# One core, attention + gated FFN + spatial FFN: w3's word conversion in other slots of a tile, and VectorE's low part of x ahead of its low part of g

## The chip, the cores and the metric

The program runs on one core of a Trainium2 chip. A core has TensorE (matrix products into PSUM), VectorE, ScalarE, GpSimd and SyncE, each with a queue of its own that it works off in order; SyncE's queue issues the DMAs here. The metric is the device time of one execution in microseconds (us), the median of several runs. Rows of the profile call the engines PE (PEld: its weight loads), DVE, ACT, POOL and SP.

## What is computed

```python
# attention: chunks of 64 tokens, 8 heads of 64, 8 x 576 tokens
scores = scale * q_c @ k_c.T;  attn = softmax(scores);  x = attn @ v_c      # -> (B, S, 512)
# first FFN (moe): w_in 512x1024, three-tap convolution over tokens, w_out 1024x512
h = relu(x @ w_in)
conv = cw[0]*h[t-1] + cw[1]*h[t] + cw[2]*h[t+1]
x2 = (h * sigmoid(conv)) @ w_out
# second FFN (moe2): w_in 512x1024 (the kernel's w3), spatial product over tokens, w_out
h = relu(x2 @ w3);  u, v = halves of h;  v_n = layernorm(v)
out = (u * (w_spatial @ v_n + b_spatial)) @ w_out
```

Some of the weights arrive as 64-bit words and are turned into fp32 on the chip.

## The kernel before

Products that need full precision are made of three fp32r products: each operand is kept as a high part (a cast on ScalarE) and a low part (operand minus high part, a subtraction, `split_lo`, line 80). So x becomes `xh` and `xl`, the gated activation g becomes `gh` and `gl`, the weights `w1h`/`w1l`, `w2h`/`w2l`, `w3h`/`w3l`.

**Phase A** does attention and the first FFN on ten tiles of 512 tokens (the last two have 256), each in `KF` = 8 slots, one per 128 columns of the hidden layer. Slot s belongs to tile s // 8. The order of every engine's queue is the order in which the Python code emits the instructions (a manual schedule). A slot of the main loop (s from 9 on) emits:

- `moe_in(s)`: TensorE makes h (12 matmuls, line 467) in one of the two PSUM buffers with the tag `h`;
- `moe_h(s)`: ScalarE's ReLU `hh` (line 487), the middle tap `c` (491), small edge columns `m` (502), then VectorE's two outer taps (506);
- one slot later `moe_tanh` (ScalarE, 515 and 517) and `moe_g` (VectorE, 521); two slots later `moe_split`: `gh` on ScalarE (529), `gl` on VectorE (80); three slots later `out`, `moe_out`: 12 matmuls with w2 into the accumulators `acc` (554). After a tile's last column block ScalarE empties the four accumulators (561); that falls at the end of slots 26, 34, 42, 50, 58 and 66.

In every fourth slot (from slot 23 to slot 55 those with s % 4 == 3) TensorE also makes the scores `s` of one attention group and the product with v, `x` or `px`, of the group before. Call this a **front slot** where the product stands at the slot's head (`front` in the code): slots 16, 20, 23, 27, 31, ..., 55, 59 and 67. There `values(s)` returns two parts: `xs[0]`, ScalarE's two casts `xh` (line 432), and `xs[1]`, VectorE's two subtractions `xl`. The product takes **both** `h` buffers of PSUM; `moe_in(s)` of the same slot writes the buffer of the product's first half, so its first matmul needs the first of the two `xl` to be done. On TensorE the order in a front slot is product, scores, `out`, `moe_in`, and then the next slot's `moe_in`.

A group's softmax runs on VectorE in the front slot and the one behind it. From slot 23 on, the attention matrix is transposed by VectorE (329) and moved by 16 small DMAs per group, `pt<-t` (line 339), on SP's queue; the product four slots later reads `pt`.

**w3's conversion** goes through `later`, an object of class `Pieces`, eight pieces of 128x512 words: `load` (a DMA into one of two `raw` buffers), `scale` (ScalarE, line 91, `nr<-raw`), `merge` (VectorE, lines 95 and 99), `split` (a cast to `w3h` on ScalarE, line 147, and GpSimd's subtraction `w3l`, line 80). Before the change a piece is scaled at the end of a slot with s % 4 == 1, merged in the next slot, and split four slots after that, ahead of the next piece's merge. Phase B (second FFN) follows and is not touched.

Lines of the main loop that matter, from before:

```python
            elif s > 2 * KF and s % 4 == 1:
                later.scale()
            elif s > 2 * KF and s % 4 == 2:
                later.split()
                weave(later.merge())
                later.load()
```

Of the kernel before, what the change touches and what calls it, by code (L numbers as in the profile page):

```python
# [22 lines left out]
KF = FF // 128  # L23
# [49 lines left out]
def attention_moe_kernel(ctx: ExitStack, tc: tile.TileContext, qT, kT, vL, vP, eye, w1, cw, w2, w3, wsp, wsr, bsp, w4, out):  # L73
# [33 lines left out]
    def weave(*lists):  # L107

        for i in range(max(map(len, lists), default=0)):
            for steps in lists:  # L110
                if i < len(steps):
                    steps[i]()
# [56 lines left out]
    def w_in_pieces(w, wh, wl, order):  # L169
        cs = [slice(f * 128, f * 128 + 128) for f in order]  # L170
        return [(w[:, :, c], KD, 128, wh[:, :, c], wl[:, :, c]) for c in cs]
# [5 lines left out]
    def phase_a(mid):  # L177
# [105 lines left out]
        def att_sm1(*halves):  # L283
            weave(*[sm1_steps(*x) for x in halves])

        def att_exp(g, j):
            _, nu = size(g)
            d = att[g]
            e = d["e", j][:, :nu, :]
            if (g, j) in ACC:  # L290

                ps, mx = d["ps"][j], d["mx", j]
                sm = d["sm", j] = ap.tile([128, 8, 1], F32, tag="sm", name="sm", bufs=4)
                for i in range(nu):
                    nc.scalar.activation(
                        out=e[:, i, :], in_=ps[:, i, :], func=AF.Exp, scale=SCALE, bias=mx[:, i, :],
                        accum_out=sm[:, i, :],
                    )
                return
            nc.scalar.activation(out=e, in_=e, func=AF.Exp, scale=SCALE)  # L300
# [42 lines left out]
        def att_sm2(*halves):  # L343
            weave(*[sm2_steps(*x) for x in halves])
# [113 lines left out]
        def moe_in(s):  # L458
            i, f = divmod(s, KF)
            xh, xl = xt[i]  # L460
            w = width(i)
            ph = ps_h.tile([128, 512], F32, tag="h", name="h")[:, :w]
            terms = ((w1h, xh), (w1l, xh), (w1h, xl))
            n = 0
            for wt, x in terms if s > KF or s == 0 else (terms[0], terms[2], terms[1]):
                for k in range(KD):
                    nc.tensor.matmul(  # L467
                        ph, wt[:, k, f * 128:(f + 1) * 128], x[:, k, :w], start=n == 0, stop=n == 11
                    )
                    n += 1  # L470
            hs[s] = ph

        def moe_hh(s):
            i, f = divmod(s, KF)
            h = mp.tile([128, WMAX + 2], F32, tag="hh", name="hh", bufs=3)
            if i:
                nc.gpsimd.tensor_copy(out=h[:, 0:2], in_=carry[:, f, :])
            hhs[s] = h
# [33 lines left out]
        def moe_tanh(s):  # L512
            _, c = gs[s]
            for dst, src, w, m in fixes.pop(s):
                nc.scalar.activation(out=dst, in_=src, func=AF.Identity, scale=w, bias=m)  # L515

            nc.scalar.activation(out=c, in_=c, func=AF.Tanh, scale=0.5)  # L517

        def moe_g(s):
            h, c = gs.pop(s)  # L520
            nc.vector.scalar_tensor_tensor(out=c, in0=c, scalar=1.0, in1=h, op0=ALU.add, op1=ALU.mult)  # L521
            gs[s] = c

        def moe_split(s):
            g = gs.pop(s)
            n = outputs(s // KF)[1]
            gh = mp.tile([128, WMAX], F32R, tag="gh", name="gh", bufs=LAG)[:, :n]
            gl = mp.tile([128, WMAX], F32R, tag="gl", name="gl", bufs=LAG)[:, :n]
            nc.scalar.copy(out=gh, in_=g)  # L529
            split_lo(nc.vector, gl, g, gh)  # L530
            gs[s] = (gh, gl)
# [3 lines left out]
        def store():  # L535
            while stores:
                dst, src = stores.pop(0)
                nc.sync.dma_start(out=dst, in_=src)
# [116 lines left out]
        def scores(s):  # L655
            if s in at:
                g = at[s]
                att_s(g)((0, 1))
                if s > 1:
                    load_qk(g + 1)  # L660
                for j in range(2):
                    if s < START:
                        todo.setdefault((s, 1), []).append((g, j))
                        todo[s + 1, 2 + j] = [(g, j)]
                        todo[s + 1, 8] = [(g, 0)]
                        todo[s + 2, 4] = [(g, 1)]
                        if g < NP:
                            todo[s + 2, 5 + j] = [(g, j)]
                    else:
                        todo[s + j, 0] = (g, j)  # L670
                        if g < NP:
                            todo[s + 1 + j, 7] = (g, j)

        def values(s):
            if s in pv_at:
                g = pv_at[s]
                xs = att_pv(g)
                load_v(g + VBUFS)
                return xs
            return (lambda: None,) * 2  # L680
# [61 lines left out]
        def out(s):  # L742
            if s - LAG0 < KF:
                moe_out(s - LAG0)
            elif s - LAG >= KF:
                moe_out(s - LAG)

        for s in range(NS + LAG):
            if s < START:
                start_slot(s)  # L750
                continue
            if s == START:
                es_st.close()
            if s == 2 * KF + 1:
                es_wf.close()
                w3p = es_b.enter_context(tc.tile_pool(name="w3p", bufs=1, side="right", reuse_waits="tile"))
                for nm in ("w3h", "w3l"):
                    wB[nm] = w3p.tile([128, KD, FF], F32R, name=nm)
                es_lp = ExitStack()
                lp = es_lp.enter_context(tc.tile_pool(name="later", bufs=1, side="right"))  # L760
                later = Pieces(lp, w_in_pieces(w3, wB["w3h"], wB["w3l"], (4, 5, 6, 7, 0, 1, 2, 3)))
                later.load()


            if s < NS:
                moe_hh(s)
            xs = ()
            tp = todo.pop((s, 7), None)
            front = pv_at.get(s, 0) >= PAIRED
            if front:  # L770
                xs = values(s)
                xs[0]()
            scores(s)
            store()
            soft = todo.pop((s, 0), None)
            if KF + 2 <= s < NS + 2:
                moe_split(s - 2)
            if xs:
                xs[1]()
            if s < NS + 1:  # L780
                moe_tanh(s - 1)
            if soft:
                att_sm1(soft)
                att_exp(*soft)
            if s < NS + 1:
                moe_g(s - 1)
            if soft:
                att_sm2(soft)
            if front:
                out(s)  # L790
            if s < NS:
                moe_in(s)
                if tp:
                    tp = att_tp(*tp)
                moe_h(s)
                if tp:
                    tp()
            if not front:
                out(s)
                for x in values(s):  # L800
                    x()
            if s == NS + LAG - 1:
                store()
            if first.wait:
                first.part(*first.wait.pop(0))
            elif s > 2 * KF and s % 4 == 1:
                later.scale()
            elif s > 2 * KF and s % 4 == 2:
                later.split()
                weave(later.merge())  # L810
                later.load()
            if s == NS - KF:
                es_at.close()
                es_lp.close()
                mid()
                x2p = es.enter_context(tc.tile_pool(name="x2p", bufs=1))
                x2s = [f for b in range(2) for f in x2_parts(b, x2p)]
                x2l = [f() for f in x2s[:2]]
                x2s = x2s[2:]
            elif NS - KF < s <= NS:  # L820
                x2l.pop(0)()
                if x2s:
                    x2l.append(x2s.pop(0)())
# [6 lines left out]
    def mid():  # L830
        wB["x"] = es_b.enter_context(tc.tile_pool(name="xB", bufs=2, side="right", reuse_waits="tile"))
# [217 lines left out]
    with tc.manual_schedule():  # L1049
        phase_a(mid)  # L1050
        phase_b()
# [59 lines left out]
```

## Time and profile before

| what | value |
|---|---|
| median of 3 runs | 924.49 us (924.35 to 924.71) |
| the profiled execution, its own time | 925.31 us |
| its span, first to last instruction | 923.5 us |
| mean granted TensorE clock | 0.994 |
| busy: PE, DVE, ACT, POOL | 897.5, 574.5, 476.9, 75.0 us |
| phase A ends, phase B's first product starts | 499.96 us |

Busy times are unions of an engine's instructions over the span. TensorE is the busiest engine by far, so the reading is about the few stretches in which it waits, who ended those waits, and what the engine named had done until then.

### The profile page before, as it was taken

To read this page: it belongs to the slowest core of one execution; us is meant where nothing else is said; L and a number is where in the kernel's file an instruction comes from. 1 tells how busy PE (TensorE), PEld (TensorE's weight loads), DVE (VectorE), ACT (ScalarE), POOL (GpSimd) and SP (SyncE) were. 2 spreads that over 40 slices of the span, in tenths; PEclk is the share of its full clock that TensorE was granted. 3 is DMA by queue.
4 is the path that set the end of the run, shared out by engine and by line. 5 is a ranking of instruction groups with operands and counts; after the bars stand their busy time and mean duration, and the time that the engine had idled before them with its cause. 6 is when DMAs were issued, how large, how long until landed. Compare 5 with 4: busy or idle time off the path is not lost.

```text
span 923.5 us, 17174 instructions
## 1 busy us (share of the span) xinstructions
PE 897.5 (97%) x6820; PEld 762.1 (83%) x6820; DVE 574.5 (62%) x1061; ACT 476.9 (52%) x1046; POOL 75.0 (8%) x200
## 2 busy tenths in 40 slices
PE   6989899999999999999999999999999999999998
PEld 5656687877777777877899999989898999989897
DVE  5795887888888787875766772734527071633522
ACT  4563777767676766676566543333324233332322
POOL 0000241001111110000011110100001000100000
PEclk9899999999999999999999999999999999999999
DMA  9551313434353533321224502030020302020001
GB/s 306 177 206 46 114 48 114 138 115 137 110 155 113 154 90 89 99 68 46 65 77 139 168 14 85 13 110 23 35 64 1 119 14 84 14 80 1 29 19 57
DMA packets 64592, 81.62 MB, mean 88 GB/s; under 512 B 7680, under 2 KB 51840, under 8 KB 64384
## 3 DMA queue, kind: packets, MB, share of 16 engines
q1 hardware_dynamic: 64512, 80.53, 27.7%
q8 instruction: 54, 0.88, 0.4%
q14 instruction: 26, 0.21, 0.1%
HBM read 54.29 MB, written 18.87 MB: 79 GB/s over the span
## 4 chain that ended last, share of the span: by engine, by line
PE 69%; DVE 15%; ACT 10%; DMA 3%; SPq 2%; issue 2%; ACTq 0%
PE pss L985 13%; PE h L467 11%; PE psu L951 11%; PE pso L1004 11%; PE psv L899 11%; PE acc L554 10%; DVE c L506 4%; DVE e L320 1%; DVE sm L311 1%; ACT x L561 1%; DVE gl L80 1%; ACT c L517 1%; ACT c L515 1%; DVE e L277 1%; ACT e L300 1%
## 5 line engine op out<-in xcount | busy, mean ns | idle before, releaser
L506 DVE SCALAR_TENSOR_TENSOR c<-hh,nr,c 128x512 f32<-128x512 f32 (+3 forms) x160 | 111.8, 699 | 41.5 <-ACT c L491 38.4
L987 DVE TENSOR_TENSOR gf<-pss,bb 128x288 f32<-128x288 f32 x64 | 29.0, 452 | 146.4 <-PE pss L985 146.4
L467 PE MATMUL h<-xh,w1h 128*128 128x512 f32 (+1 forms) x320 | 84.8, 387 | 7.2 <-DVE xl L80 6.3
L467 PE MATMUL h<-xh,w1l 128*128 128x512 f32 (+1 forms) x320 | 81.5, 377 | 0.0
L467 PE MATMUL h<-xl,w1h 128*128 128x512 f32 (+1 forms) x320 | 81.4, 376 | 0.0
L989 ACT CAST gth<-gf 128x288 fp32r<-128x288 f32 x64 | 27.7, 433 | 96.3 <-DVE gf L988 96.3
L467 PEld LDWEIGHTS h<-xh,w1h 128*128 128x128 f32 x320 | 56.1, 190 | 23.6 <-DVE xl L80 10.0
L985 PE MATMUL pss<-wsh,vl 128*128 128x288 f32 x256 | 75.4, 295 | 0.0
L985 PE MATMUL pss<-wsh,vh 128*128 128x288 f32 x256 | 75.4, 294 | 0.0
L985 PE MATMUL pss<-wsl,vh 128*128 128x288 f32 x256 | 75.3, 294 | 0.0
L554 PE MATMUL acc<-gh,w2h 128*128 128x512 f32 (+2 forms) x288 | 74.8, 379 | 0.1
L554 PE MATMUL acc<-gh,w2l 128*128 128x512 f32 (+2 forms) x288 | 71.5, 370 | 0.0
L554 PE MATMUL acc<-gl,w2h 128*128 128x512 f32 (+2 forms) x288 | 71.4, 370 | 0.0
L521 DVE SCALAR_TENSOR_TENSOR c<-c,hh 128x512 f32<-128x512 f32 (+2 forms) x80 | 50.7, 634 | 27.9 <-ACT c L517 27.4
L467 PEld LDWEIGHTS h<-xh,w1l 128*128 128x128 f32 x320 | 57.8, 191 | 12.2
L467 PEld LDWEIGHTS h<-xl,w1h 128*128 128x128 f32 x320 | 57.7, 191 | 12.1
L80 DVE TENSOR_TENSOR gl<-c,gh 128x512 fp32r<-128x512 f32 (+2 forms) x72 | 50.9, 706 | 19.9 <-ACT gh L529 19.9
L487 ACT ACTIVATE hh<-h 128x512 f32<-128x512 f32 (+1 forms) x80 | 43.6, 545 | 30.4 <-PE h L467 30.2
L515 ACT ACTIVATE c<-hh,m,nr 128x1 f32<-128x1 f32 x112 | 37.6, 385 | 42.0 <-DVE c L506 42.0
L554 PEld LDWEIGHTS acc<-gl,w2h 128*128 128x128 f32 x288 | 50.8, 188 | 10.2
L554 PEld LDWEIGHTS acc<-gh,w2l 128*128 128x128 f32 x288 | 50.8, 188 | 9.9
L955 ACT ACTIVATE u<-psu 128x288 f32<-128x288 f32 x64 | 26.4, 413 | 62.5 <-PE psu L951 62.5
(126 smaller groups left out, 1876.3 us busy)
## 6 DMA issues: line engine op xcount, KB each, us to landing
raw<-in_w_dram SPq DMA_DIRECT2D x26, 512.0 KB, 5.6
x2f<-x2d SPq DMA_DIRECT2D x32, 288.0 KB, 3.2
q<-in_qT_dram SPq DMA_DIRECT2D x16, 512.0 KB, 4.5
k<-in_kT_dram SPq DMA_DIRECT2D x16, 512.0 KB, 5.5
out_dram<-o SPq DMA_DIRECT2D x32, 256.0 KB, 2.1
pt<-t SPq DMA_DIRECT2D x160, 32.0 KB, 1.8
v<-in_vP_dram SPq DMA_DIRECT2D x8, 512.0 KB, 5.4
v<-in_vL_dram SPq DMA_DIRECT2D x10, 256.0 KB, 3.7
```

The lines of the kernel that those rows point to most:

```text
L80: eng.tensor_tensor(out=lo, in0=full, in1=hi, op=ALU.subtract)
L467: nc.tensor.matmul(ph, wt[:, k, f * 128:(f + 1) * 128], x[:, k, :w], start=n == 0, stop=n == 11)
L487: nc.scalar.activation(out=h[:, b:], in_=ph, func=AF.Relu)
L506: nc.vector.scalar_tensor_tensor(out=c[:, a:z], in0=h[:, o + a + step:o + z + step], scalar=cws[:, tap, f:f + 1], in1=c[:, a:z], op0=ALU.m ...
L515: nc.scalar.activation(out=dst, in_=src, func=AF.Identity, scale=w, bias=m)
L521: nc.vector.scalar_tensor_tensor(out=c, in0=c, scalar=1.0, in1=h, op0=ALU.add, op1=ALU.mult)
L554: nc.tensor.matmul(accs[m], w[:, f, m * 128:(m + 1) * 128], x, start=f == 0 and j == 0, stop=f == KF - 1 and j == len(terms) - 1,)
L899: nc.tensor.matmul(ps, x[:, k, sl], w[:, k, DV:], start=i == 0, stop=i == 11)
L951: nc.tensor.matmul(ps[:, :HB], w[:, k, d * 128:(d + 1) * 128], x[:, k, t], start=i == 0, stop=i == 11)
L985: nc.tensor.matmul(o, a[:, ds], w, start=i == 0, stop=i == len(mm) - 1)
L987: nc.vector.tensor_tensor(out=gf, in0=o, in1=bb[:, t], op=ALU.add)
L1004: nc.tensor.matmul(ps, x[:, k, sl], w[:, k, :], start=i == 0, stop=i == 11)
```

## The change

Two edits in the slot loop. First, in a front slot, VectorE's two `xl` are emitted ahead of `moe_split`, so ahead of `gl`; ScalarE's own order (`xh`, `xh`, `gh`) stays. Second, `later`'s steps move: `scale` from slots s % 4 == 1 to s % 4 == 0, `merge` and `load` from s % 4 == 2 to s % 4 == 1, `split` stays in s % 4 == 2 and now takes the piece merged one slot earlier.

```diff
             soft = todo.pop((s, 0), None)
+            if xs:
+                xs[1]()
             if KF + 2 <= s < NS + 2:
                 moe_split(s - 2)
-            if xs:
-                xs[1]()
...
+            elif s > 2 * KF and s % 4 == 0:
+                later.scale()
             elif s > 2 * KF and s % 4 == 1:
-                later.scale()
+                weave(later.merge())
+                later.load()
             elif s > 2 * KF and s % 4 == 2:
                 later.split()
-                weave(later.merge())
-                later.load()
```

VectorE's queue from the end of a slot with s % 4 == 1 to the front slot two later; `c<-hh,nr,c` are the taps, `c<-c,hh` is `moe_g`, `raw` and `nr` the merge. Before:

```order
L506 SCALAR_TENSOR_TENSOR c<-hh,nr,c 128x512 x2
L80 TENSOR_TENSOR gl<-c,gh 128x512
L521 SCALAR_TENSOR_TENSOR c<-c,hh 128x512
L506 SCALAR_TENSOR_TENSOR c<-hh,nr,c 128x512 x2
L95 TENSOR_SCALAR raw<-raw 128x512
L99 SCALAR_TENSOR_TENSOR nr<-nr,raw 128x512
L80 TENSOR_TENSOR gl<-c,gh 128x512
L80 TENSOR_TENSOR xl<-x,xh 128x2x256 x2
L271 TENSOR_REDUCE mx<-s 128x8
```

The same place of the changed kernel:

```order
L506 SCALAR_TENSOR_TENSOR c<-hh,nr,c 128x512 x2
L95 TENSOR_SCALAR raw<-raw 128x512
L99 SCALAR_TENSOR_TENSOR nr<-nr,raw 128x512
L80 TENSOR_TENSOR gl<-c,gh 128x512
L521 SCALAR_TENSOR_TENSOR c<-c,hh 128x512
L506 SCALAR_TENSOR_TENSOR c<-hh,nr,c 128x512 x2
L80 TENSOR_TENSOR xl<-x,xh 128x2x256 x2
L80 TENSOR_TENSOR gl<-c,gh 128x512
L271 TENSOR_REDUCE mx<-s 128x8
```

The merge has gone up by one slot, and `xl` stands directly behind the taps, with `gl` behind it.

SP's queue at the same place, with the semaphores that each DMA waits for; the last of the 16 `pt` stands first. Before:

```order
L339 DMA pt<-t 32x256 [waits DMAHW5_49]
L132 DMA raw<-in_w_dram 128x4x128 [waits DMAHW6_49]
L227 DMA v<-in_vL_dram 128x2x256 [waits DMAHW7_49,PE_49]
L230 DMA v<-in_vL_dram 64x2x256 [waits DMAHW0_49]
L217 DMA q<-in_qT_dram 128x4x256 [waits DMAHW2_49,PE_49]
```

The same place of the changed kernel:

```order
L339 DMA pt<-t 32x256 [waits DMAHW5_49]
L132 DMA raw<-in_w_dram 128x4x128 [waits DMAHW6_49,DVE_49,Activation_49]
L227 DMA v<-in_vL_dram 128x2x256 [waits DMAHW7_49,PE_49]
L230 DMA v<-in_vL_dram 64x2x256 [waits DMAHW0_49]
L217 DMA q<-in_qT_dram 128x4x256 [waits DMAHW2_49,PE_49]
```

The order is unchanged, but the load of a piece now waits for VectorE: its `raw` buffer is the one that the merge of the same slot reads.

## Rows read from the trace of the kernel before

**Rows 1.** Waits: engine line <- releaser: us in total, times, longest us.

```profile
PE h L467 <- DVE xl L80: 6.3, 9, 1.0
...
PEld acc L554 <- ACT x L561: 2.3, 8, 0.3
```

**Rows 2.** Window from slot 27's product to slot 55's: length, busy us.

```profile
207.64:387.03 179.39, 174.41 (x1569) 138.49 (x1569) 146.33 (x236) 124.39 (x281) 22.82 (x64) 1.00 0.40 118
```

**Rows 3.** Timeline of PE, slots 35 and 39: start, us, [idle <-releaser].

```profile
258.48 1.16 PE L416 MATMUL x<-pt,v 64*64 64x64 f32 x64
...
264.73 1.19 PE L467 MATMUL h<-xh,w1h 128*128 128x512 f32 x4 [0.97 <-DVE xl L80]
...
284.46 1.16 PE L416 MATMUL x<-pt,v 64*64 64x64 f32 x64
...
290.01 1.20 PE L467 MATMUL h<-xh,w1h 128*128 128x512 f32 x4 [0.45 <-DVE xl L80]
```

**Rows 4.** Timeline of PE, slots 55 and 59.

```profile
387.03 1.16 PE L416 MATMUL x<-pt,v 64*64 64x64 f32 x64
...
391.96 1.10 PE L467 MATMUL h<-xh,w1h 128*128 128x512 f32 x4
...
411.60 1.16 PE L416 MATMUL x<-pt,v 64*64 64x64 f32 x64
...
417.10 1.20 PE L467 MATMUL h<-xh,w1h 128*128 128x512 f32 x4 [0.44 <-DVE xl L80]
```

**Rows 5.** Timeline of PE and ACT, slot 67.

```profile
457.69 1.11 ACT L432 CAST xh<-x 128x512 fp32r<-128x512 f32 x2
...
460.20 0.73 PE L467 MATMUL h<-xh,w1h 128*128 128x256 f32 x4 [0.89 <-DVE xl L80]
```

**Rows 6.** Timeline of DVE, slots 34 to 39.

```profile
260.52 0.42 DVE L95 TENSOR_SCALAR raw<-raw 128x512 uint32<-128x512 uint32 x1
...
263.38 0.69 DVE L80 TENSOR_TENSOR gl<-c,gh 128x512 fp32r<-128x512 f32 x1 [1.71 <-ACT gh L529]
263.99 1.28 DVE L80 TENSOR_TENSOR xl<-x,xh 128x512 fp32r<-128x512 f32 x2
...
283.74 0.69 DVE L521 SCALAR_TENSOR_TENSOR c<-c,hh 128x512 f32<-128x512 f32 x1 [0.85 <-ACT c L517]
285.04 1.54 DVE L506 SCALAR_TENSOR_TENSOR c<-hh,nr,c 128x512 f32<-128x512 f32 x2 [0.61 <-ACT c L491]
286.50 1.52 DVE L95 TENSOR_SCALAR raw<-raw 128x512 uint32<-128x512 uint32 x1
288.06 0.70 DVE L99 SCALAR_TENSOR_TENSOR nr<-nr,raw 128x512 uint32<-128x512 uint32 x1
288.67 0.69 DVE L80 TENSOR_TENSOR gl<-c,gh 128x512 fp32r<-128x512 f32 x1
```

**Rows 7.** Timeline of ACT, slots 35 to 39.

```profile
261.73 1.10 ACT L432 CAST xh<-x 128x512 fp32r<-128x512 f32 x2
...
278.08 0.67 ACT L515 ACTIVATE c<-hh,m,nr 128x1 f32<-128x1 f32 x2 [1.99 <-DVE c L506]
...
285.79 1.06 ACT L432 CAST xh<-x 128x512 fp32r<-128x512 f32 x2
```

**Rows 8.** Timeline of POOL: the splits of slots 34 and 38.

```profile
261.93 1.29 POOL L80 TENSOR_TENSOR w3l<-nr,w3h 128x512 fp32r<-128x512 f32 x1 [3.40 <-ACT w3h L147]
...
285.97 1.77 POOL L80 TENSOR_TENSOR w3l<-nr,w3h 128x512 fp32r<-128x512 f32 x1 [1.46 <-ACT w3h L147]
```

**Rows 9.** Timeline of DVE, slot 11, beside GpSimd's split of a w2 piece.

```profile
107.50 1.78 DVE L80 TENSOR_TENSOR gl<-c,gh 128x512 fp32r<-128x512 f32 x1
```

**Rows 10.** SP's queue behind slot 35, and the page's DMA issues (KB, us to landing).

```profile
269.92 11.61 SPq L339 DMA_DIRECT2D pt<-t  x16
281.58 0.64 SPq L132 DMA_DIRECT2D raw<-in_w_dram  x1
...
pt<-t SPq DMA_DIRECT2D x160, 32.0 KB, 1.8
```

## The prediction

> **What bounds the kernel now.** I read the waits of TensorE first, because it is the busiest engine. After the start-up one wait is left in phase A that costs it anything: the first matmul of `h` waits for VectorE's `xl`, nine times, 6.3 us together [rows 1]. Then I looked where these nine lie. Seven are in the stretch from slot 27's product to slot 55's, in which TensorE is idle for 179.39 − 174.41 = 4.98 us [rows 2]; the other two are in slots 59 (0.44 us, [rows 4]) and 67 (0.89 us, [rows 5]). 4.98 + 0.44 + 0.89 = 6.31, so nothing else stops TensorE there. All nine are front slots, the slots in which the product with v holds both `h` buffers until `xl` has been subtracted.
>
> The timeline shows two kinds. In slot 35, a front slot right behind the emptying of the accumulators, the wait is 0.97 us; in slot 39, in the middle of a tile, 0.45 us [rows 3]. Slot 55 is the control: no piece of w3 is converted any more, and `h` starts without a wait [rows 4]. From its product to the next one are 411.60 − 387.03 = 24.57 us [rows 4]. That is four slots with TensorE never held up by `xl`, and I take it as the floor.
>
> Why is `xl` late? In slot 35, VectorE sits idle for 1.71 us waiting for `gh`, then does `gl`, then `xl` at 263.99 [rows 6]. But `xl` doesn't need `gh`; it needs `xh`, whose two casts take 1.10 us from 261.73, so the first was there at about 262.3 [rows 7]. Half of the wait is queue order alone. In slot 39, ScalarE is in time (`xh` from 285.79, the first done at about 286.3, [rows 7]), and VectorE is late: behind the taps, which end at 286.5, stand the merge (1.52 + 0.70 us) and `gl` (0.69), and `xl` can only follow at 289.3 [rows 6].
>
> **The change part by part.**
>
> *`xl` ahead of `gl`.* No instruction is added; two change places. In slot 35 the first `xl` starts at about 262.3, when its cast is done, and ends 1.28 / 2 = 0.64 us later, at 262.95 [rows 6, 7]. TensorE was free for `h` at 264.73 − 0.97 = 263.76 [rows 3]. So the wait goes, with 0.8 us to spare. `gl` comes behind the second `xl`, at about 263.6, which is the time that it has now (263.38), because it had to wait for `gh` anyway. Its reader is `out` of slot 36, which stands behind two `moe_in` on TensorE, over 5 us on; being late costs nothing there. Behind `gl` stand the maxima and the softmax, and they come about 1 us earlier.
>
> *The merge one slot earlier.* In slot 39 the taps are now followed by `xl` directly: start 286.5, first one done at 287.15, where TensorE needs it at 290.01 − 0.45 = 289.56 [rows 3, 6]. The wait of 0.45 us goes, with over 2 us to spare. The merge itself (0.42 + 0.70 = 1.12 us when nothing holds it, [rows 6]) goes in behind the taps of slot 37. What hides it there: VectorE waits for ScalarE in slot 38 for 0.85 us ahead of `moe_g` and for 0.61 us ahead of the taps [rows 6], 1.46 us in all. Behind the merge are queued `gl` (read by TensorE a slot later), `moe_g` and the taps; the taps wait for ScalarE's `c`, not for the merge. I cost it at nothing. If that cover were gone, it would be 1.12 us for each of eight pieces.
>
> *The merge away from GpSimd's split.* Its first instruction takes 0.42 us in slot 34 and 1.52 in slot 38, and in slot 38 GpSimd's split runs from 285.97 to 287.74, over its start [rows 6, 8]. So 1.1 us of VectorE is lost wherever the two meet. In the new place GpSimd has only edge columns to copy. GpSimd's split now meets `xl` instead. No row here shows an `xl` fully under a split. Another instruction does: `gl` in slot 11 took 1.78 us instead of 0.69, beside a split [rows 6, 9]. From below `xl` is not held at all. From above it waits until the split is over: in slot 39 until 287.74, first `xl` done at 288.4, still before 289.56; in slot 35 until 263.22, done at 263.86, 0.1 us after TensorE wants it [rows 3, 8]. I take nothing, and at most 0.3 us with the restart in each of four slots like slot 35.
>
> The Trainium skill (GPSIMD Engine Reference, Specifications) says that GpSimd shares its SBUF interfaces with VectorE and that this hurts instructions with two SBUF inputs or in a two-port mode. The rows on the merge and on `gl` agree; `xl` has one input in PSUM, so by that rule it would not be held, and the sum would be that of the lower bound.
>
> *The scale one slot earlier.* One activation on ScalarE leaves slot 37 for slot 36, where ScalarE waits for VectorE up to 1.99 us at a time [rows 7]. Nothing on TensorE's path.
>
> *The load.* Its DMA now waits for the merge of its own slot. Before it went out at 281.58, right behind the 16 `pt` [rows 10]; now it goes out when the merge ends. The taps of slot 37 end at 283.74 − 0.85 − 0.69 = 282.2 (`moe_g`'s start less its wait and a `gl`, [rows 6]), so the merge ends at about 283.3. Behind it stand v, q and k, which wait for slot 39's product at 284.46 anyway [rows 3]. Nothing.
>
> *Sum.* Slots 27 to 55 are seven stretches of four slots: 179.39 − 7 × 24.57 = 7.40 us over the floor, more than the 4.98 us of idle time, since each restart also costs the pipeline some tenths. Of that I leave in place the wait of `acc` for the emptying of the accumulators, at most 0.3 us at the four slots that have it [rows 1], about half of it: −0.6. So 6.8 us. Slot 59 gives 0.44 and slot 67 gives 0.89 (its first `xh` is there at about 458.2, so `xl` at 458.9, against 460.20 − 0.89 = 459.31, [rows 5]). Together 8.1 us. The profiled execution took 925.31 us (span 923.5); it becomes 917.2. The median of the runs is 0.82 us below the profiled one, so the prediction is **916.4 us**.
>
> **The rivals.**
>
> *A: the tile-end slots keep their wait.* If in slots 27, 35, 43, 51, 59 and 67 something else holds `xl` as long (ScalarE, which has just emptied the accumulators, or the split), only the three mid-tile slots gain. They are 0.45 us of idle plus restart each, some 0.7: 2.2 us, so 922.3. With half of the tile-end waits gone, about 919.5. Against it: VectorE's idle time in slot 35 is put down to `gh`, not `xh` [rows 6].
>
> *B: the attention matrix becomes late.* 16 `pt` take 11.61 us to issue from 269.92, and land 1.8 us after the last: 283.3, for a product at 284.46 [rows 3, 10]. Counted from slot 35's product that is 24.87 us; the floor is 24.57. If the first `pt` doesn't go out earlier than now, each tile-end stretch keeps 0.3 us, four of them 1.2 us: 917.6. For it: 1.1 us of slack against 1.4 us to be gained. Against it: the softmax in front of it starts about 1 us earlier by the new order.
>
> *C: slower, or no gain.* The merge now stands ahead of slot 38's `gl` and `moe_g`, which are already behind TensorE. If it is not absorbed and delays ScalarE's ReLU of slot 38, the product of slot 39 has no buffer. Eight merges at 1.12 us are 9.0 us against 8.1 gained: 925.4, the same. At the held length (1.52 + 0.70 = 2.22) they are 17.8, and 934.2. It decides at about 1.25 us on the path per merge (0.2% over). Against it: the tanh and the ReLU wait for the taps that stand ahead of the merge, and slot 38 has 1.46 us of idle VectorE.
>
> *D: it does nothing*, because another wait as long stands right behind `xl`: 924.5. Slot 55, where `h` starts at once, speaks against it.
>
> **How the numbers follow.** Two kernels less than 0.2% (1.85 us) apart can't be told from each other here. The forecast, with B inside it, has 75%: 914.8 to 918; its lower end is the whole 7.40 with 0.3 us more for the restarts in slots 59 and 67, 9.3 in all, and a little of the waits ahead of slot 27. A has 14%, 918 to 922.5. D and the mild end of C have 7%, the hard end of C 4%. The range 914.8 to 919.3 takes in the forecast and the nearer half of A. Faster: the forecast and nearly all of A, 0.88; the same 0.08; slower 0.04.
>
> **What the profile after would show.** Right: no row "h <- xl" among TensorE's waits, or well under 1 us of it; 24.6 to 24.9 us from product to product in slots 27 to 55; L95 always 0.42 us in phase A; `gl` behind `xl`, at about the old time in slot 35. The prediction is wrong if TensorE waits anew for `px` or `x` (B or C), if `xl` takes more than 0.7 us under the split, or if ScalarE's `xh` comes later than now.

## The result, and the profile after

The changed kernel took 916.43 us (median of 4, 915.59 to 917.24) beside 924.42 us before: a ratio of 0.9910, with a 95% interval of 0.9898 to 0.9923. The forecast was 916.4 us. Four more runs of it in a later comparison gave 0.9907 (0.9893 to 0.9922).

Two lines of the changed kernel's page, busy time per engine and the shares of the chain of work that ended last:

```profile
PE 893.3 (98%) x6820; PEld 761.6 (83%) x6820; DVE 569.7 (62%) x1061; ACT 476.9 (52%) x1046; POOL 74.1 (8%) x200
...
PE 89%; DVE 4%; ACT 4%; DMA 1%; issue 1%; SPq 1%; ACTq 0%
```

The same line of the chain before:

```profile
PE 69%; DVE 15%; ACT 10%; DMA 3%; SPq 2%; issue 2%; ACTq 0%
```

The chain now runs 89% of the span over TensorE, where it was 69%. The window from slot 27's product to slot 55's, the same stretch as in [rows 2] (length, then each engine's busy us, PE first):

```profile
207.11:379.12 172.01, 172.01 (x1569) 139.28 (x1568) 142.90 (x236) 124.92 (x282) 21.74 (x64) 1.00 0.43 126
```

TensorE is busy for all of it. 172.01 / 7 = 24.57 us from product to product, the floor that slot 55 showed before. The gain here is 179.39 − 172.01 = 7.38 us. Behind slot 55's product the profiled span has 913.8 − 379.12 = 534.68 us left, and had 923.5 − 387.03 = 536.47: 1.79 us, for slots 59 and 67. The remaining 0.53 us of the 9.7 between the two profiled spans lie ahead of slot 16, where no instruction has moved: the first `h` started 0.38 us earlier and its matmuls took less time. I don't count it as the change's: a second trace of the changed kernel (e8) has slot 27's product 2.01 us later than this one, at 209.12.

TensorE's timeline in slots 35 and 39 of the changed kernel:

```profile
256.26 1.16 PE L416 MATMUL x<-pt,v 64*64 64x64 f32 x64
...
261.19 1.10 PE L467 MATMUL h<-xh,w1h 128*128 128x512 f32 x4
...
280.83 1.16 PE L416 MATMUL x<-pt,v 64*64 64x64 f32 x64
...
285.76 1.10 PE L467 MATMUL h<-xh,w1h 128*128 128x512 f32 x4
```

Where 0.97 and 0.45 us of waiting stood in [rows 3], nothing stands. What VectorE did there, in its timeline:

```profile
259.65 1.29 DVE L80 TENSOR_TENSOR xl<-x,xh 128x512 fp32r<-128x512 f32 x2 [1.76 <-ACT xh L432]
260.86 0.68 DVE L80 TENSOR_TENSOR gl<-c,gh 128x512 fp32r<-128x512 f32 x1
...
278.48 0.42 DVE L95 TENSOR_SCALAR raw<-raw 128x512 uint32<-128x512 uint32 x1
...
282.78 1.28 DVE L80 TENSOR_TENSOR xl<-x,xh 128x512 fp32r<-128x512 f32 x2
283.98 0.68 DVE L80 TENSOR_TENSOR gl<-c,gh 128x512 fp32r<-128x512 f32 x1
```

And GpSimd, in its own, the splits of the same two slots:

```profile
259.21 1.30 POOL L80 TENSOR_TENSOR w3l<-nr,w3h 128x512 fp32r<-128x512 f32 x1 [3.31 <-ACT w3h L147]
...
282.25 1.77 POOL L80 TENSOR_TENSOR w3l<-nr,w3h 128x512 fp32r<-128x512 f32 x1 [1.37 <-ACT w3h L147]
```

Read three things. In slot 35 `xl` waits for `xh` itself, and the first of the two is done at 260.3, 0.9 us ahead of `h`. In slot 39 `xl` starts as the taps end and runs under GpSimd's split, to the end of it (282.25 to 284.02), without taking longer. And `gl` starts as the split ends (283.98), so it too takes 0.68 us.

### The profile page after: what moved, and what is told of

Same layout as the page of the kernel before. It is cut to its first block, busy times and chain, and to the rows that moved or that the text cites. A ratio compares the mean times of both kernels' runs of the same rounds, so it can differ in the third digit from the quotient of the medians.

```text
span 913.8 us, 17158 instructions
## 1 busy us (share of the span) xinstructions
PE 893.3 (98%) x6820; PEld 761.6 (83%) x6820; DVE 569.7 (62%) x1061; ACT 476.9 (52%) x1046; POOL 74.1 (8%) x200
## 4 chain that ended last, share of the span: by engine, by line
PE 89%; DVE 4%; ACT 4%; DMA 1%; issue 1%; SPq 1%; ACTq 0%
PE acc L554 20%; PE h L467 19%; PE pss L986 13%; PE psu L952 11%; PE pso L1005 11%; PE psv L900 11%; PE s L256 2%; DVE c L506 1%; PE x L416 1%; PE px L397 1%; DMA raw<-in_w_dram 1%; ACT c L491 1%; DMA idt<-in_eye_dram 1%; ACT hh L487 1%; ACT c L517 1%
## 5 line engine op out<-in xcount | busy, mean ns | idle before, releaser
L491 ACT ACTIVATE c<-hh,nr 128x512 f32<-128x512 f32 (+2 forms) x80 | 54.6, 682 | 6.9
```

Of the source, the lines that this page charges most:

```text
L491: nc.scalar.activation(out=c, in_=h[:, o:o + n], func=AF.Copy, scale=cws[:, 1, f:f + 1])
```

## The experiments

### Each edit alone

`xl` ahead of `gl`, w3 in its old slots:

```diff
+            if xs:
+                xs[1]()
             if KF + 2 <= s < NS + 2:
                 moe_split(s - 2)
-            if xs:
-                xs[1]()
```

> Only the order of VectorE in front slots is changed (xl ahead of gl); w3's conversion stays in its old slots. My theory: xl waits for nothing but xh and the place in the queue, so this edit alone takes nearly all of the gain. Slots 27, 35, 43, 51, 59, 67: no wait. Slots 31, 39, 47: xl starts when the merge ends (288.7 in the old time), is done 0.64 us later, against 289.56: no wait either, or under 0.2 us each. So 916.5 to 917.5 us, 0.991 to 0.9925 of before. Rival, both edits are needed: the mid-tile slots keep 0.45 us and restart each, 918.5 us or more. L95 takes 1.5 us in slots 22, 30, 38, 46 as before by both.

Measured: 918.89 us, ratio 0.9943 (0.9931 to 0.9955). TensorE's matmuls wait for `xl` in none of the nine slots any more, as I expected (three of its weight loads still do, for 0.3 us each), but part of the gain is missing: 2.5 us by the medians, 3.0 by the ratios. TensorE's timeline with the products of slots 27 and 51:

```profile
206.30 1.16 PE L416 MATMUL x<-pt,v 64*64 64x64 f32 x64
...
356.10 1.64 PE L416 MATMUL x<-pt,v 64*64 64x64 f32 x63
```

What the weight loads of products wait for (us in total, times, longest):

```profile
PEld x L416 <- ACT hh L487: 1.7, 6, 0.4
...
PEld x L416 <- ACT c L517: 1.1, 3, 0.4
```

And the merge in slot 38, in VectorE's timeline:

```profile
283.11 1.52 DVE L95 TENSOR_SCALAR raw<-raw 128x512 uint32<-128x512 uint32 x1
```

From slot 27 to slot 51 are 149.80 us, 2.4 over 6 × 24.57; all seven stretches, to slot 55's product, are 3.1 over. The product itself has become late: it needs both `h` buffers, the second is freed by ScalarE's ReLU `hh`, and the ReLU stands behind a tanh that waits for VectorE's taps. The changed kernel has the first of these two rows as well (1.5 us, 4 times), but not the second. VectorE is later here than in the changed kernel: the merge stands ahead of `xl` again, and in slot 38 it is held. My expectation was wrong in its time and right in its first step; the rival's time was nearer, but not its reason.

w3's steps moved, `gl` still ahead of `xl`:

```diff
-            if xs:
-                xs[1]()
             if KF + 2 <= s < NS + 2:
                 moe_split(s - 2)
+            if xs:
+                xs[1]()
```

(against the changed kernel)

> Only w3's steps are moved; gl stays ahead of xl. My theory: the tile-end slots (27, 35, 43, 51, 59, 67) wait for gh on ScalarE, which the merge has nothing to do with, so they keep 0.4 to 1.0 us each; slots 31, 39, 47 lose their wait. TensorE's row h <- xl goes from 6.3 us to about 4.9 in 6 waits; 922.0 to 922.6 us, ratio about 0.9975. In slots 31, 39, 47 gl now meets GpSimd's split and takes about 1.0 us in place of 0.69. Rival, it is the merge and the split that hold xl: most of the 8 us comes back, 918 us or less.

Measured: 0.9978 (0.9964 to 0.9993) of before, 2.0 us less by the ratio and 3.1 by the medians (921.07 us; the twelve runs scatter from 919.89 to 927.01). TensorE's row of waits:

```profile
PE h L467 <- DVE xl L80: 4.4, 6, 1.0
```

`gl` in slot 39, in VectorE's timeline:

```profile
285.23 0.88 DVE L80 TENSOR_TENSOR gl<-c,gh 128x512 fp32r<-128x512 f32 x1 [0.83 <-ACT gh L529]
```

Six waits are left, those of the tile-end slots, where `gl` waits for `gh`; the three mid-tile ones are gone. `gl` meets the end of the split and takes 0.2 us more. The waits went as expected. By the ratios the two edits alone give 5.3 and 2.0 of 8.3 us; by the traces, from slot 27's product to slot 55's, 4.3 (175.13 us) and 3.2 (176.21) of 7.4. The intervals are too wide to say whether the gains simply add. The mid-tile waits go with either edit.

### What the second edit is worth: the place, or the split

Two kernels keep e1's order and the merge in its old slot, and take GpSimd's split, with the cast `w3h` that it follows on ScalarE, away from it. The first:

```diff
+            elif s > 2 * KF and s % 4 == 0:
+                later.split()
             elif s > 2 * KF and s % 4 == 2:
-                later.split()
                 weave(later.merge())
                 later.load()
```

> The kernel of e1 (xl first, scale and merge in their old slots), but with GpSimd's split of a piece in slots s % 4 == 0 in place of s % 4 == 2, so that the merge meets no split. It asks which half of the second edit is worth the 2.5 us that e1 lacks: that the merge is not held (1.1 us in slots 30, 38, 46), or that it stands a slot earlier. In e1 the first weights of a product wait for tanh and ReLU on ScalarE, and the six stretches from slot 27's to slot 51's product are 2.4 us over 6 x 24.57. If the hold is what costs: L95 at 0.42 us, the stretches that end in slots 35, 43, 51 fall from 25.3 to 24.6 or so, and the time is within 0.1% of the changed kernel's. If the place costs: they stay at 25 or more and the time stays near 919 us. The split now stands ahead of the next slot's two-input instructions and can hold the taps or gl there by up to 1.1 us, which would show as a longer L506 or gl in slots 28, 32, 36, ... .

Measured: 920.20 us, 0.9961 (0.9949 to 0.9973), no better than e1; the profiled execution, 924.89 us, was the longest of the twelve. The merge was no longer held, but the taps were, in slot 36 and every fourth slot like it. In VectorE's timeline:

```profile
279.34 2.33 DVE L506 SCALAR_TENSOR_TENSOR c<-hh,nr,c 128x512 f32<-128x512 f32 x2
```

beside this split in GpSimd's:

```profile
279.05 1.30 POOL L80 TENSOR_TENSOR w3l<-nr,w3h 128x512 fp32r<-128x512 f32 x1 [1.47 <-ACT w3h L147]
```

2.33 us in place of 1.50: the hold had moved, and so this run by itself settles nothing but that. The second puts the split into the front slot, behind `gl`:

```diff
             if KF + 2 <= s < NS + 2:
                 moe_split(s - 2)
+            if s > 2 * KF + 1 and s % 4 == 3 and s < NS - KF:
+                later.split()
...
             elif s > 2 * KF and s % 4 == 2:
-                later.split()
                 weave(later.merge())
```

> Again e1's kernel (xl first, merge in its old slot), but GpSimd's split is emitted in the front slot right behind gl, as e6 does it for w2, so that it should hold neither the merge, nor the taps (as in e7), nor gl. It is the cleaner form of e7's question. If the hold of 1.1 us is what e1 lacks: the stretches between products fall to 24.6 us and the time is that of the changed kernel, 916 to 917 us. If it is the merge's place in the slot ahead of the front slot (1.1 us of VectorE on the way to the ReLU that frees the h buffer): stretches of 24.9 to 25.4 us remain and 918.5 to 919 us. In between, both: 917 to 918 us.

Measured: 915.57 us, 0.9906 (0.9890 to 0.9921), the changed kernel's time. TensorE's timeline with the products of slots 27 and 51:

```profile
206.56 1.16 PE L416 MATMUL x<-pt,v 64*64 64x64 f32 x64
...
354.38 1.20 PE L416 MATMUL x<-pt,v 64*64 64x64 f32 x63
```

VectorE's timeline with the merge of slot 38 and `gl` of slot 39:

```profile
282.11 0.42 DVE L95 TENSOR_SCALAR raw<-raw 128x512 uint32<-128x512 uint32 x1
...
284.37 1.46 DVE L80 TENSOR_TENSOR gl<-c,gh 128x512 fp32r<-128x512 f32 x1
```

147.82 us for the six stretches are 0.4 over the floor (0.7 for all seven), although the merge stands where it stood before and `gl` is held by 0.8 us in slot 39. So the merge does not have to leave its old slot: with the split and its cast elsewhere that slot costs 0.7 us at most.

Which of the two that moved gave the time back is not parted by this run. In slot 39 the merge is 1.10 us shorter than in e1 and `gl` 0.78 us longer, so VectorE wins 0.32 us. In slot 35 the cast no longer stands ahead of `xh`. ScalarE's timeline in e1, and VectorE's `xl` there:

```profile
258.80 0.63 ACT L147 CAST w3h<-nr 128x512 fp32r<-128x512 f32 x1
259.31 1.09 ACT L432 CAST xh<-x 128x512 fp32r<-128x512 f32 x2
...
259.95 1.29 DVE L80 TENSOR_TENSOR xl<-x,xh 128x512 fp32r<-128x512 f32 x2 [0.70 <-ACT xh L432]
```

`xl` of the same slot in e10:

```profile
258.99 1.29 DVE L80 TENSOR_TENSOR xl<-x,xh 128x512 fp32r<-128x512 f32 x2 [0.19 <-ACT xh L432]
```

`xl` waits for `xh` in both, 0.51 us less without the cast. The stretches move alike: from slot 39 to 43 they fall from 24.94 to 24.57 us, from 43 to 47 from 25.40 to 24.87. By this estimate, from one trace of each, the hold has the smaller and the cast the larger part of what e10 takes off. The cast is not needed for the floor, though: the changed kernel keeps it ahead of `xh`. And the hold does cost something: e7 and e10 differ in the split's slot alone, the cast is out of `xh`'s way in both, and e7, where the taps are held in each stretch, is 0.55% (5 us) slower. How much of e1's loss is the hold, the merge's slot or the cast stays open.

### How much the merge's new place hides

Two or four more instructions behind each merge, which leave the piece as it is:

```diff
                 weave(later.merge())
+                if later.merged:
+                    f = later.merged[-1][0]
+                    for _ in range(2):    # 4 in the second kernel
+                        nc.vector.scalar_tensor_tensor(out=f, in0=f, scalar=1.0, in1=f, op0=ALU.mult, op1=ALU.max)
                 later.load()
```

> The changed kernel with two more VectorE instructions behind each merge, each of the merge's second kind (two inputs in SBUF, 128x512, 0.69 us, about 0.63 in a row) that leave the piece as it is: eight times 1.3 us more work at the place of the merge. My theory: VectorE's pauses hide it; the old xl spare (2.3 us in slot 39, 0.9 in slot 35) is not used up: 0 to 1 us slower than the changed kernel. Rival C, the merge's place lies on the chain of VectorE and ScalarE that frees the h buffer: all of it shows, 8 x 1.3 = 10 us.

> The same with four more, 8 x 2.6 us. My theory: the delay passes slot 38's pauses by 2.1 us; in the mid-tile slots the softmax starts 2.1 us later and the ReLU that frees the next product's buffer (ready 0.76 us before the product now) comes 1.3 us late, in the tile-end slots ScalarE's 1.76 us hide most: 4 to 6 us slower than the changed kernel, with a new wait of the product's matmuls for hh. Rival C: 8 x 2.6 = 21 us. If VectorE has far more slack than that: 0.

Measured: 0.9917 (0.9896 to 0.9939) with two, 1.0047 (1.0030 to 1.0063) with four. TensorE's timeline with the products of slots 27 and 51, with two more:

```profile
205.85 1.16 PE L416 MATMUL x<-pt,v 64*64 64x64 f32 x64
...
354.64 1.46 PE L416 MATMUL x<-pt,v 64*64 64x64 f32 x63
```

The same with four more:

```profile
205.25 1.69 PE L416 MATMUL x<-pt,v 64*64 64x64 f32 x63
...
363.85 1.66 PE L416 MATMUL x<-pt,v 64*64 64x64 f32 x63
```

With two, six stretches take 1.4 us more than the floor; with four, 11.2. Two take 1.42 us, so 8.5 us were added over the six; four take 2.87, so 17.2. Two are nearly hidden (0.6 us slower than the changed kernel by the ratios; I expected 0 to 1), and four cost some 13 us, more than twice what I expected. VectorE's timeline around slot 38 with four:

```profile
284.05 2.87 DVE L813 SCALAR_TENSOR_TENSOR nr<-nr 128x512 f32<-128x512 f32 x4
...
288.04 2.58 DVE L506 SCALAR_TENSOR_TENSOR c<-hh,nr,c 128x512 f32<-128x512 f32 x2
```

and ScalarE's:

```profile
286.95 0.62 ACT L147 CAST w3h<-nr 128x512 fp32r<-128x512 f32 x1 [0.91 <-DVE nr L813]
```

The piece comes late to ScalarE's cast, the split starts late and meets the taps, and those take 2.58 us in place of 1.54: the hold comes back. That is a part of the loss, not all of it. With two the taps of slot 38 are held as well (2.44 us), but those of slot 34 are not (1.53); with four those are too (2.45). Rival C's full price (21 us) did not come either, but the place has an edge: of 8.5 us added, 1.4 show, of 17.2 some two thirds.

### The attention matrix (rival B)

```diff
                             dst, src = pt[o0:o0 + 32, qh, :nu, :], t[s0:s0 + 32, kh, :nu, :]
-                            nc.sync.dma_start(out=dst, in_=src)
+                            m = nu // 2 if qh == kh == 0 else nu
+                            nc.sync.dma_start(out=dst[:, :m, :], in_=src[:, :m, :])
+                            if m < nu:
+                                nc.sync.dma_start(out=dst[:, m:, :], in_=src[:, m:, :])
```

> The changed kernel with the attention matrix moved in 20 DMAs per group in place of 16 (two of each eight are cut in halves; same bytes). This is rival B: the issue on SP's queue takes 0.73 us per DMA, so the last lands 2.9 us later. In the changed kernel it lands about 1.2 us before the product of slot 39 and 1.6 before that of slot 43. If that slack is all there is, products wait 1.3 to 1.7 us in slots 27 to 67: 9 to 14 us slower than the changed kernel, with the product waiting for the DMA pt<-t. If issue time is not what sets the landing: no change.

Measured: 916.91 us, 0.9900 (0.9881 to 0.9920): no loss. My number for an issue was wrong. The second transpose of slot 35's group in the changed kernel, in VectorE's timeline:

```profile
272.13 0.71 DVE L329 STREAM_TRANSPOSE t<-e 128x512 f32<-128x512 f32 x1
```

and the group's 16 issues on SP's queue:

```profile
266.20 11.62 SPq L339 DMA_DIRECT2D pt<-t  x16
```

SP waits for the second half: from 272.84 to 277.82 it issues eight, 0.62 us each, and the 11.62 us, which my expectation of 0.73 us each spread over 16, hold a pause of 1.6 us. Ten of them ended at 279.30, 1.5 us later; only slot 67's product then waited for `pt`, 1.19 us. The chain ahead of a product goes through the second transpose and the eight issues behind it, not through 16, and in slot 39 has at least 1.5 us of slack.

### A version that goes further

The same hold exists for w2's pieces in slots 9 to 16 ([rows 9]). On top of the changed kernel, their split goes behind `gl`:

```diff
             if KF + 2 <= s < NS + 2:
                 moe_split(s - 2)
+            if first.wait:
+                first.part(*first.wait.pop(0))
             if s < NS + 1:
                 moe_tanh(s - 1)
...
-            if first.wait:
-                first.part(*first.wait.pop(0))
-            elif s > 2 * KF and s % 4 == 0:
+            if s > 2 * KF and s % 4 == 0:
```

> On top of the changed kernel: in slots 9 to 16 the split of a w2 piece (cast on ScalarE, subtraction on GpSimd) is emitted right behind moe_split and ahead of the tanh, so that GpSimd starts when gl is running or done. Theory: a VectorE instruction with two inputs in SBUF and GpSimd's subtraction hold each other off. Then gl takes 0.69 us in slots 10 to 16 in place of 1.36 to 1.79, VectorE and ScalarE are earlier by 0.7 to 1.1 us there, and TensorE's waits of 1.58 us for e and 1.24 us for pt near 105 to 111 us shrink to under 1 us each: 914.5 to 915.7 us, a ratio to the changed kernel of 0.998 to 0.999. Rival: the loss only moves to the next two-input instructions (moe_g, the normalisation, the taps), which then take 1.0 us or more beside the split, and the time stays within 0.1%.

Measured: 914.16 us, 0.9891 (0.9878 to 0.9904). VectorE's `gl` over 95 to 160 us (min/median/max in ns, first and last start) in the changed kernel:

```profile
L80 DVE TENSOR_TENSOR gl<-c,gh x9: 678/1366/1789, 100.3 to 154.4; 128x512 fp32r<-128x512 f32 x9
```

The same in the second run of this one:

```profile
L80 DVE TENSOR_TENSOR gl<-c,gh x10: 680/684/692, 100.9 to 159.3; 128x512 fp32r<-128x512 f32 x10
```

TensorE's timeline with its wait for the softmax, in the changed kernel:

```profile
105.72 0.63 PE L356 MATMUL tp<-idt,e 128*128 128x128 f32 x4 [1.58 <-DVE e L320]
```

and in the second run of this one:

```profile
105.64 0.63 PE L356 MATMUL tp<-idt,e 128*128 128x128 f32 x4 [0.42 <-DVE e L320]
```

`gl` is never held, and 1.16 us of a wait are gone; the next one, 1.24 us for `pt`, stays. To size the gain, both went on one chip:

> The changed kernel itself, beside e6's on one chip: 0.991 of before by every theory.

> e6's kernel again, beside the changed one: its trace showed TensorE's wait for e fall from 1.58 to 0.41 us and gl at 0.69 us throughout, so 1.0 to 1.5 us (0.1 to 0.2%) below the changed kernel. If the 2.3 us seen between them before were mostly chance between chips: within 0.5 us.

916.36 us (0.9907) against 915.34 us (0.9900, 0.9881 to 0.9918): 1.0 us by the medians, near the 1.16 that the trace shows, and too little for these intervals to tell apart. Its medians are the lowest here; that it is faster than the changed kernel is not settled by the times.

## Why the prediction was right

**The floor and term 1.** The stretches did fall to 24.57 us each. I had left 0.6 us in place for the emptying of the accumulators; in slot 35 it no longer costs anything: the weight loads of `acc` still wait (1.4 us in 5 places, before 2.3 in 8), but the first four `acc` matmuls of slot 35 take 1.20 us, as in slot 39; before they took 1.40. ScalarE starts to empty the accumulators 0.33 us behind slot 35's product there, before 0.83. 7.38 us measured, 6.8 forecast.

**Slots 59 and 67.** 1.79 us measured, 0.44 + 0.89 = 1.33 forecast; the restarts that I had left out make up the rest. The term was slightly too small. So the trace has 9.2 us for the two terms where 8.1 were forecast, while the medians, whose runs scatter by 1.6 us, came to 8.0. That the last digits agree is luck.

**`xl` ahead of `gl`.** Right, and by itself 5.3 us by the ratio (e1). The spare in slot 35 was forecast at 0.8 us and is 0.9; in slot 39 it was over 2 and is 2.3.

**The merge one slot earlier.** I gave this step the mid-tile waits of 0.45 us. They do go by it alone (e2), but they go by the other edit alone too (e1). That the place costs nothing was right: the merge's 1.12 us are hidden, and so is most of 1.4 us more (e3).

**The merge away from GpSimd's split.** This is the step that I under-read. I wrote that 1.1 us of VectorE is lost where the two meet, and gave it no term of its own. e1 has no matmul left that waits for `xl` and still takes 918.89 us, outside the 914.8 to 918 that I gave the forecast. A late VectorE reaches TensorE by a second way, which I named only under C: through the softmax, the taps and the ReLU that frees the product's buffer. How much of it is the hold, the merge's slot or the cast ahead of `xh`, these runs do not part (e7, e10). The sum was right because the floor was taken from slot 55, where neither a merge nor a split runs, and so took in all of it.

**What the split does to `xl`.** The lower bound was right: `xl` ran under a split in 0.64 us each, the length that it has without one, and the split of slot 35 took its usual 1.30 us beside it. The Trainium skill (GPSIMD Engine Reference, Specifications) names two inputs in SBUF or a two-port mode as what collides; `xl` has one input in PSUM, and the trace agrees with it: `gl` and the taps, with two inputs in SBUF, were held, `xl` was not. L95 was held with one input; that it runs in such a mode would fit its 0.42 us, but no run here shows it.

**The rivals.** A did not come: `xh` was in time. B took the 11.61 us of the 16 issues as one block behind the first, but a pause for the second transpose lies in it (e4); and the first `pt` now goes out 9.94 us behind slot 35's product (266.20 − 256.26), before 11.44, so B's condition did not come. (Its 24.87 us should read 24.85.) C's chain is real, as e1 and e3 show, but starts beyond what the change adds.

## What to carry to other kernels

Take the floor for a repeated stretch from a repetition in which the suspected work is absent, and subtract whole stretches; the printed waits alone were 2.4 us short here. When an instruction is a buffer's last reader, look at what stands ahead of it in its queue without being its input. And where GpSimd works beside VectorE, see which instruction a split meets: moved into another slot it held the taps there (e7); emitted behind `gl`, where reads from PSUM follow, it cost less: 0.8 us at `gl` in every second front slot (e10), nothing in e6.

## What the runs showed of the hardware that was not expected

The hold works both ways and goes to whichever came second. With the taps running, the split took 1.77 us in place of 1.30 [rows 8]; with the split running, the taps took 2.33 (e7) to 2.58 us (e3) for two in place of 1.54, `gl` up to 1.79 in place of 0.69, and L95 1.52 in place of 0.42. An instruction that started behind a split waited for all of the rest of it: L95 in slot 38 began at 286.50 and ended at 288.02, 0.28 us after the split [rows 6, 8].
